# Three hand-placed reorderings in the start of a fused soft-cap attention and max-out MLP: a w2 product ahead of the next transposes, three w1 parts ahead of the first crossbar transpose, fill units behind the second quad's values

## The chip, the cores and the metric

The kernel runs on one core of one Trainium2 chip. The metric is the device time of one execution in microseconds (us). Five runs of the kernel before gave 344.70, 344.70, 343.57, 343.85 and 345.86 us, a median of 344.7. Beside these, one execution was profiled: every duration and every wait below comes from its trace. A page of that trace names lines of the kernel (L426 is line 426) and engines: PE does matrix multiplies, PEld loads their weights, DVE, ACT and POOL work on elements, SP issues DMAs.

## The reference

Attention over 8 batches of 12 heads, 448 rows and 64 columns, with capped scores; its output, laid out as 3584 rows of 768, goes through two up-projections, of which the larger is kept, and one down-projection:

```python
scores = cap * np.tanh(scale * (q @ k.T) / cap)
attn = np.exp(scores); attn = attn / attn.sum(-1)
x = attn @ v
h1, h2 = x @ w1, x @ w2
out = np.maximum(h1, h2) @ w_out
```

The kernel uses max(h1, h2) = h2 + relu(h1 - h2). So it needs two matrices that depend on the weights alone: wd = w1 - w2, for the relu part, and wm = w2 @ w_out, which takes x straight to the h2 part of the output. It computes out = x @ wm + relu(x @ wd) @ w_out.

## The kernel before

**Attention.** Two heads make a pair, two pairs a quad; there are 24 quads, t = 0 to 23, three to a batch. Three pairs are one group g for loading: `load` brings k, q and v, `cast` turns them into bf16 (on DVE or POOL), and then k and q have to be transposed into the tile `qkT`. For g = 0 and 1 PE does it, a pair at a time (`transposes(i)`, L281 and L282, and a copy on DVE, L283). From g = 2 on one DMA does it for the whole group, through the crossbar: `cross(g)`, L287, issued by SP when POOL has finished the group's casts. `cross(2)` serves quad 3 on, and `cross(3)` is wanted first by `scores(4, 1)`.

For a quad, `scores(t, p)` multiplies k with q (L309, L312) and has ACT take the tanh (L313). Parts 0 and 1 have three score tiles each, j = 0 to 2, part 2 has one, and each tile is two banks of PSUM. `ex` takes the exp (L318). `total(t)` sums it with ones as weights (L352, L356, later L359), and DVE turns the sums into reciprocals `inv` (L361, L363, L365). `values(t)` multiplies with v (L375, L381), and `normalize(t)` scales the result on DVE into `xT` (L396). The pool `s_psum` has two buffers, for score tiles and totals alike; `v_psum` has one, for values and, where the code says `v_psum`, for a third score tile. `expo` has two buffers, so `ex(2, 0)` must wait until `total(0)` and `values(0)` have read what quad 0 left.

**The fill.** Everything else that PE does is cut into units of one matmul and put into a queue, `fill_q`. `F(n)` in the hand-written order runs n units at that place. The first 144 units make wm: `(c, T)` is eight transposes of slice c of w2 (L241) and a copy on DVE into `w2T` (L243), and `(c, half)` is eight matmuls with w_out (L252) and a copy on DVE (L256). After them come the units of `moe(b)`, one generator per batch: 48 units of the up-projection with wd (L408, each six followed by the relu on DVE, L413), and then 14 units (six L423 with wm, eight L426) for each half row block of the output, followed by a copy on DVE (L429). `moe(b)` is put into the queue only when its batch's last quad is normalized, so `F` finds the queue empty if the units run out before. Inside the loop over t = 3 to 23 a quad asks for 47 units. `moe(0)` has 132 units, and `moe(1)` is put in at the end of t = 5.

**wd.** w1 comes as twelve parts of 256 KB, `load_w1(c, part)` (L228), issued by SP; w2 comes through POOL's queue (L220). `subtract(c, part, eng)` (L232) makes wd, part 0 for the first four column blocks f, part 1 for the last four. POOL has c = 2 to 5 of part 0 ahead of `cast(3, "k")` and `cast(3, "q")`, and c = 0 to 2 of part 1 behind them; DVE has the rest.

**The queues.** Every engine takes its instructions in the order of the code. SP's order around the change is: q and k of group 2, v of group 1, two parts of w1, `cross(2)`, four parts of w1, k and q of group 3, six parts of w1 (part 1), and, later in the code, `cross(3)`, v of groups 2 and 3, k and q of groups 4 and 5.

Of the kernel before, what the change touches and what calls it, by code (L numbers as in the profile page):

```python
# [10 lines left out]
def kernel(  # L11
# [22 lines left out]
    KC, FC = DM // P, DF // P  # L34
# [40 lines left out]
    def flat(g):  # L75
        return kqf[g % 2].rearrange("p n j c -> p n (j c)")
# [22 lines left out]
    def half(b):  # L99
        return slice(0, 64) if b % 2 == 0 else slice(64, P)  # L100
# [8 lines left out]
    def raw_of(g, what):  # L109
        if (g, what) not in raw:  # L110
            raw[g, what] = raw_tile(what)
        t = raw[g, what]
        m = t[:, : 2 * L * NJ * D].rearrange("p (h c) -> p h c", c=NJ * D)
        l = t[:, 2 * L * NJ * D :].rearrange("p (h d) -> p h d", d=D)
        return t, m, l
# [28 lines left out]
    def cast(eng, g, what, n0=0, n1=L, halves=(0, 1)):  # L144

        b = g * L // NP
        x, m, l = raw_of(g, what)
        if what == "v" and g < NT:

            x = x[:, : L * S].rearrange("p (n c) -> p n c", c=S)  # L150
            for h in halves:
                r = slice(64 * h, 64 * h + 64)
                for a in range(2):
                    eng.tensor_copy(
                        vp[g % 2][64 * a : 64 * a + 64, h::2, :, :].rearrange("p n j d -> p n (j d)"),
                        x[r, :, NJ * D * a : NJ * D * (a + 1)],
                    )
                eng.tensor_copy(vl[g % 2][r, :, r], x[r, :, 2 * NJ * D :])  # L158
            return
        if what == "v":  # L160
            eng.tensor_copy(  # L161
                vp[g % 2][:, 2 * n0 : 2 * n1, :, :].rearrange("p h j d -> p h (j d)"), m[:, 2 * n0 : 2 * n1, :]
            )
            for par in range(2):
                r = slice(64 * par, 64 * par + 64)
                eng.tensor_copy(vl[g % 2][r, n0:n1, r], l[r, n0:n1, :])
            return
        if g < NT:

            x = x[:, n0 * S : n1 * S].rearrange("p (n c) -> p n c", c=S)  # L170
            if what == "q":
                eng.tensor_copy(flat(g)[:, n0:n1, Q0 : Q0 + S], x)
                return
            eng.tensor_copy(flat(g)[:, n0:n1, : NJ * P], x[:, :, : NJ * P])
            for par in range(2):
                r = slice(64 * par, 64 * par + 64)
                eng.tensor_copy(kf[g % 2][r, n0:n1, 3, r], x[r, :, NJ * P :])
            return
        o = b % 2 if what == "q" else 0
        t = (kf if what == "k" else qf)[g % 2]  # L180
        eng.tensor_copy(
            t[:, n0:n1, o : o + NJ, :].rearrange("p n j (h d) -> p n h j d", h=2),
            m[:, 2 * n0 : 2 * n1, :].rearrange("p (n h) (j d) -> p n h j d", h=2, d=D),
        )
        if what == "q":
            eng.tensor_copy(
                t[half(b), n0:n1, 3 * (1 - o), :],
                l[half(b), 2 * n0 : 2 * n1, :].rearrange("p (n h) d -> p n (h d)", h=2),
            )
        else:  # L190
            for par in range(2):
                r = slice(64 * par, 64 * par + 64)
                eng.tensor_copy(t[r, n0:n1, 3, r], l[r, n0:n1, :])
# [70 lines left out]
    def qkT_of(g):  # L264
        if g not in qkT:
            qkT[g] = stage.tile([P, L, 8, P], bf16, name="qkT")
        return qkT[g]

    def transposes(i):

        g, n = divmod(i, L)
        ps = mm_psum.tile([P, 512], f32, name="mm").bitcast(bf16)
        x = flat(g)[:, n, :]

        todo = [(j * D, (j % 3) * P + (j // 3) * 64) for j in range(6)]
        odd = i // NP % 2
        todo += [(Q0 + j * D, Q0 + (64 * j if not odd else 0 if j == 6 else 64 + 64 * j)) for j in range(R7)]
        for c, to in todo:
            for a in range(2):
                r = slice(64 * a, 64 * a + 64)  # L280
                nc.tensor.transpose(ps[r, to : to + 64], x[r, c : c + D], ident[r, r])  # L281
        nc.tensor.transpose(ps[:, NJ * P : Q0], x[:, NJ * P : Q0], ident)  # L282
        nc.vector.tensor_copy(qkT_of(g)[:, n, :, :].rearrange("p j c -> p (j c)")[:, : Q0 + S], ps[:, : Q0 + S])  # L283
# [12 lines left out]
    def scores(t, p, last=None, js=None):  # L296

        if (t, p) not in tanh:
            tanh[t, p] = att.tile([P, 2 * NJ, S], bf16, name="tanh")
        for j in js or range(NJ if p < 2 else 1):  # L300
            s = two_banks(last if last and j == NJ - 1 else s_psum)
            for m in range(2):
                i = 2 * t + (p if p < 2 else m)
                g = i // L
                k0 = qkT[g][:, i % L, :, :].rearrange("p j c -> p (j c)")
                o = Q0 + (64 * (i // NP % 2) if g >= NT else 0)
                qTn = k0[:, o : o + S]
                if p == 2:
                    nc.tensor.matmul(s[:, m, :S], k0[:, 3 * P : 4 * P], qTn)  # L309
                else:  # L310
                    r = slice(64 * m, 64 * m + 64)
                    nc.tensor.matmul(s[:, m, :S], k0[r, j * P : (j + 1) * P], qTn[r, :])  # L312
            nc.scalar.activation(tanh[t, p][:, 2 * j : 2 * j + 2, :], s[:, :, :S], AF.Tanh, scale=scale / cap)  # L313

    def ex(t, p):
        n = 2 * NJ if p < 2 else 2
        expo[t, p] = att.tile([P, n, S], bf16, name=f"expo{p}", bufs=2)
        nc.scalar.activation(expo[t, p], tanh[t, p][:, 0:n, :], AF.Exp, scale=float(cap))  # L318

    def e_of(t, ab, j):  # L320
        return expo[t, ab][:, 2 * j : 2 * j + 2, :]
# [24 lines left out]
    def total(t):  # L346

        ss = two_banks(s_psum)[:, 0, :]
        if t < NS:
            for j in range(NJ):  # L350
                for ab, h, r in HEADS:
                    nc.tensor.matmul(  # L352
                        ss[r, :S], ones[:, :32], e_of(t, ab, j)[:, h, :], start=(j == 0), stop=False
                    )
            for ab, h, r in HEADS:
                nc.tensor.matmul(ss[r, :S], ones2[:, h, :32], expo[t, 2][:, ab, :], start=False, stop=True)  # L356
        else:
            for ab, h, r in HEADS:
                nc.tensor.matmul(ss[r, :S], ones[:, :32], esum[t][:, 2 * ab + h, :], start=True, stop=True)  # L359
        st = att.tile([P, NB, 32], f32, name="st", bufs=1)  # L360
        nc.vector.transpose(st.rearrange("p b c -> p (b c)"), ss[:, :S])  # L361
        rs = att.tile([P, NB, 1], f32, name="rs", bufs=2)
        nc.vector.reciprocal(rs, st[:, :, 0:1])  # L363
        inv[t] = att.tile([P, S], f32, name="inv", bufs=2)
        nc.vector.transpose(inv[t].rearrange("p (b c) -> p b c", c=32), rs.to_broadcast([P, NB, 32]))  # L365
# [88 lines left out]
    def F(n):  # L454
        rate[1] += n * rate[0]
        while rate[1] >= 1 and fill_q:
            g = fill_q[0]
            if g is not rate[2]:
                rate[2] = g
                next(g)  # L460
            rate[1] -= 1
            try:
                next(g)
            except StopIteration:
                fill_q.pop(0)
        if not fill_q:
            rate[1] = 0.0
# [30 lines left out]
    def w2wo(*parts):  # L498
        for c, half in parts:
            fill_q.append(turn_w2(c) if half is None else premultiply(c, half))  # L500

    T = None
    w2wo((0, T), (1, T), (0, 0), (2, T), (1, 0), (2, 0), (0, 1), (1, 1), (3, T), (2, 1), (3, 0), (4, T), (3, 1))
    w2wo((4, 0), (5, T), (4, 1), (5, 0), (5, 1))

    fill_const(nc.vector, 0)
# [34 lines left out]
    cast(nc.gpsimd, 2, "k")  # L541
    cast(nc.gpsimd, 2, "q")
    cast(nc.gpsimd, 1, "v", halves=(1,))
    scores(0, 2)
    ex(0, 2)
    F(28)
    scores(1, 0, v_psum)
    ex(1, 0)
    F(28)
    scores(1, 1, v_psum)  # L550
    ex(1, 1)
    F(24)
# [1 line left out]
    cast(nc.vector, 0, "v", halves=(0,))  # L554
    scores(1, 2)
    ex(1, 2)
    for c in range(2):
        load_w1(c, 0)
    cross(2)
    for c in range(2, KC):  # L560
        load_w1(c, 0)
    load(3, "k")
    load(3, "q")
# [4 lines left out]
    x0 = values(0)  # L568
    scores(2, 0, js=(2,))
    ex(2, 0)  # L570
    transposes(5)
    total(0)
    F(8)
    scores(2, 1, js=(0, 1))
    normalize(0, x0)
    F(4)
    scores(2, 1, js=(2,))
    cast(nc.vector, 1, "v", halves=(0,))
    F(4)
    scores(2, 2)  # L580
    ex(2, 1)
    F(8)
    total(1)
    normalize(1, values(1))
    F(2)

    scores(3, 0, v_psum)
    ex(2, 2)
# [11 lines left out]
    load(3, "v")  # L600
    extra(4)
    extra(5)
    F(4)
    for c in range(2):
        subtract(c, 0, nc.vector)
    total(2)
# [88 lines left out]
```

## Time and profile before

| what | us |
|---|---|
| median of five runs | 344.7 |
| the profiled execution, its own time | 344.41 |
| its span, first to last instruction | 342.6 |
| PE busy in the span | 323.6 (94%) |
| ACT busy | 277.2 (81%) |
| DVE busy | 232.1 (68%) |
| POOL busy | 107.2 (31%) |

The granted clock of PE was 1.00 of full speed over the span. The profile has several views. The busy row gives each engine's share of the span. A table of stretches gives the same for any part of it. A timeline lists one engine's instructions in order of time: the start, the time that a run of equal instructions took, the engine, line and tile names, the count and, in brackets, how long the engine had been idle before and what ended that. The DMA view gives, for each issue, the time from the issue to the landing of its data.

### The profile page before, as it was taken

What the parts mean: (1) busy time and instruction counts of PE and PEld (TensorE: products, weight loads), DVE (VectorE), ACT (ScalarE), POOL (GpSimd) and SP (SyncE); (2) the same over time, 40 slices, a digit from 0 to 9 for tenths busy, and PEclk for the clock granted to TensorE, in tenths of its full rate; (3) what the DMA queues carried; (4) which work ended last, traced back from release to release, by engine and by line L of the source; (5) the groups of instructions that cost most, each with busy time, mean ns of one, the idle gap of its engine ahead of it and who ended that gap; (6) DMA issues with size and microseconds to landing.
All of it is one profiled execution on the core that took longest, in us unless ns stands there. A gap on an engine that the chain in (4) does not pass through costs nothing.

```text
span 342.6 us, 6835 instructions
## 1 busy us (share of the span) xinstructions
PE 323.6 (94%) x2722; PEld 163.3 (48%) x2722; DVE 232.1 (68%) x417; ACT 277.2 (81%) x241; POOL 107.2 (31%) x180
## 2 busy tenths in 40 slices
PE   3799969799999999999999999999999999999995
PEld 1555424345444554455445554445445544555563
DVE  4546765587887677677686668777776877874321
ACT  2999969789999999899989999999989999900000
POOL 8334667274134214403412441342144130000000
PEclk9999999999999999999999999999999999999999
DMA  7999799999996879686986689749955920012022
GB/s 217 199 238 302 192 265 272 231 250 232 185 279 175 209 196 277 161 174 140 265 229 126 125 222 309 170 130 232 294 118 142 227 78 27 0 48 92 2 92 92
DMA packets 106047, 61.78 MB, mean 180 GB/s; under 512 B 62624, under 2 KB 101024, under 8 KB 106016
## 3 DMA queue, kind: packets, MB, share of 16 engines
q1 hardware_dynamic: 102144, 58.21, 67.1%
q0 software_dynamic: 3872, 3.15, 5.9%
q8 instruction: 21, 0.34, 0.4%
q14 instruction: 10, 0.08, 0.1%
HBM read 42.47 MB, written 11.01 MB: 156 GB/s over the span
## 4 chain that ended last, share of the span: by engine, by line
PE 80%; DMA 10%; DVE 4%; POOL 2%; SPq 2%; issue 1%; POOLq 0%; DVEq 0%
PE mm L426 22%; PE mm L408 19%; PE mm L423 16%; PE v L375 6%; PE s L312 6%; DMA gT<-in_moe_w_dram 3%; DMA vr<-in_v_dram 3%; DMA qr<-in_q_dram 2%; PE v L312 2%; PE v L381 2%; PE s L309 2%; PE mm L252 2%; PE s L359 2%; DMA qkT<-kqf 2%; SPq L133 1%
## 5 line engine op out<-in xcount | busy, mean ns | idle before, releaser
L318 ACT ACTIVATE expo<-tanh 128x2688 bf16<-128x2688 bf16 (+1 forms) x72 | 140.3, 1950 | 0.7 <-PE s L352 0.5
L313 ACT ACTIVATE tanh<-s 128x896 bf16<-128x896 f32 x123 | 107.4, 914 | 20.9 <-PE s L312 17.8
L426 PE MATMUL mm<-wo_sb,gT 128*128 128x384 bf16 x448 | 86.0, 327 | 0.0
L408 PE MATMUL mm<-xT,wd_sb 128*128 128x448 bf16 x384 | 78.2, 353 | 1.0 <-DVE gT L413 0.7
L423 PE MATMUL mm<-wm_sb,xT 128*128 128x384 bf16 x336 | 66.0, 327 | 0.0
L429 DVE COPY osb<-mm 128x384 f32<-128x384 f32 x56 | 31.1, 555 | 44.2 <-PE mm L426 43.8
L426 PEld LDWEIGHTS <-gT 128*128 128x128 bf16 x448 | 42.3, 98 | 34.6 <-issue 8.5
L408 PEld LDWEIGHTS <-wd_sb 128*128 128x128 bf16 x384 | 35.8, 98 | 39.5 <-issue 9.0
L413 DVE TENSOR_SCALAR gT<-mm 128x448 bf16<-128x448 f32 x64 | 39.4, 621 | 20.5 <-PE mm L408 20.3
L423 PEld LDWEIGHTS <-xT 128*128 128x128 bf16 x336 | 31.8, 98 | 25.9 <-issue 5.9
L655 POOL COPY mark<-inv 1x1 f32<-1x1 f32 x18 | 3.2, 177 | 130.6 <-DVE inv L365 114.9
L313 ACT ACTIVATE tanh<-v 128x896 bf16<-128x896 f32 x45 | 41.6, 925 | 0.0
L375 PE MATMUL v<-expo,vp 128*32 128x448 bf16 x576 | 35.9, 353 | 0.0
L312 PE MATMUL s<-qkT 64*128 64x448 bf16 x198 | 28.3, 363 | 6.4 <-DMA qkT<-kqf 4.4
L396 DVE TENSOR_TENSOR xT<-v,inv 128x448 bf16<-128x448 f32 x48 | 27.7, 619 | 3.0 <-DVE inv L365 0.5
L338 DVE TENSOR_TENSOR esum<-expo 128x896 bf16<-128x896 bf16 x40 | 27.8, 695 | 0.0
L340 DVE TENSOR_TENSOR esum<-esum,expo 128x896 bf16<-128x896 bf16 x40 | 25.7, 643 | 0.8
L361 DVE STREAM_TRANSPOSE st<-s 128x448 f32<-128x448 f32 x24 | 15.6, 649 | 14.7 <-PE s L359 12.6
L336 DVE TENSOR_TENSOR esum<-esum,expo 64x896 bf16<-64x896 bf16 x40 | 24.6, 616 | 1.1
L312 PEld LDWEIGHTS <-qkT 64*128 64x128 bf16 x288 | 10.5, 95 | 28.4 <-issue 16.0
L375 PEld LDWEIGHTS <-vp 128*32 128x32 bf16 x576 | 15.4, 97 | 10.6 <-DVE vl L158 0.4
L161 POOL CAST vp<-vr 128x1152 bf16<-128x1152 f32 x14 | 16.0, 1144 | 10.3 <-DMA vr<-in_v_dram 10.1
(66 smaller groups left out, 261.7 us busy)
## 6 DMA issues: line engine op xcount, KB each, us to landing
kr<-in_k_dram SPq DMA_DIRECT2D x14, 576.0 KB, 7.1
qr<-in_q_dram SPq DMA_DIRECT2D x14, 576.0 KB, 7.5
vr<-in_v_dram SPq DMA_DIRECT2D x14, 576.0 KB, 4.9
out_dram<-osb SPq DMA_DIRECT2D x20, 384.0 KB, 4.1
out_dram<-osb SPq DMA_DIRECT2D x16, 192.0 KB, 3.7
osb<-in_moe_w_dram SPq DMA_DIRECT2D x8, 256.0 KB, 5.9
gT<-in_moe_w_dram POOLq DMA_DIRECT2D x12, 128.0 KB, 9.2
wo_sb<-in_moe_w_out_dram POOLq DMA_DIRECT2D x4, 384.0 KB, 8.7
```

Of the source, the lines that this page charges most:

```text
L312: nc.tensor.matmul(s[:, m, :S], k0[r, j * P : (j + 1) * P], qTn[r, :])
L313: nc.scalar.activation(tanh[t, p][:, 2 * j : 2 * j + 2, :], s[:, :, :S], AF.Tanh, scale=scale / cap)
L318: nc.scalar.activation(expo[t, p], tanh[t, p][:, 0:n, :], AF.Exp, scale=float(cap))
L338: nc.vector.tensor_add(d, e_of(t, ab, 0), e_of(t, ab, 1))
L340: nc.vector.tensor_add(d, d, e_of(t, ab, 2))
L375: nc.tensor.matmul(ps[r, :S], vp[g % 2][:, 2 * n + h, j, u::2], e_of(t, ab, j)[:, h, :], start=(j == 0), stop=False,)
L396: nc.vector.tensor_mul(x_of(t, u), ps[:, u, :S], inv[t])
L408: nc.tensor.matmul(ps[:, :S], wd_sb[:, c, f * P : (f + 1) * P], x[:, c, cs], start=(c == 0), stop=(c == KC - 1))
L413: nc.vector.tensor_relu(g[f // FH][:, f % FH, cs], ps[:, :S])
L423: nc.tensor.matmul(ps[:, : DM // 2], x[:, c, ts], wm_sb[:, c, hs], start=(c == 0), stop=False)
L426: nc.tensor.matmul(ps[:, : DM // 2], g[f // FH][:, f % FH, ts], wo_sb[:, f, hs], start=False, stop=(f == FC - 1))
L429: nc.vector.tensor_copy(osb[:, hs], ps[:, : DM // 2])
```

## The change

All edits are in the hand-written order; no instruction is added or removed.

- In the list of w2 products `(0, 0)` stands ahead of `(1, T)`.
- Eight fill units are taken ahead of `scores(0, 2)`; the next `F(28)` becomes 16, and the one after it 32.
- Three parts of w1 instead of two are issued ahead of `cross(2)`.
- `total(0)` stands ahead of `transposes(5)`.
- The fill between the scores of quad 2 changes from 4 and 4 units to 6 and 2.
- The eight units ahead of `total(1)` go, and the fill behind `normalize(1)` grows from 2 to 10.
- The fill ahead of the first two subtracts on DVE and `total(2)` grows from 4 to 8.

```diff
-    w2wo((0, T), (1, T), (0, 0), (2, T), (1, 0), ...
+    w2wo((0, T), (0, 0), (1, T), (2, T), (1, 0), ...
...
+    F(8)
     scores(0, 2)
     ex(0, 2)
-    F(28)
+    F(16)
     scores(1, 0, v_psum)
     ex(1, 0)
-    F(28)
+    F(32)
     scores(1, 1, v_psum)
...
-    for c in range(2):
+    for c in range(3):
         load_w1(c, 0)
     cross(2)
-    for c in range(2, KC):
+    for c in range(3, KC):
         load_w1(c, 0)
...
+    total(0)
     transposes(5)
-    total(0)
     F(8)
     scores(2, 1, js=(0, 1))
     normalize(0, x0)
-    F(4)
+    F(6)
     scores(2, 1, js=(2,))
     cast(nc.vector, 1, "v", halves=(0,))
-    F(4)
+    F(2)
     scores(2, 2)
     ex(2, 1)
-    F(8)
     total(1)
     normalize(1, values(1))
-    F(2)
+    F(10)
 
     scores(3, 0, v_psum)
...
-    F(4)
+    F(8)
     for c in range(2):
         subtract(c, 0, nc.vector)
     total(2)
```

## The prediction

> **What bounds the kernel now.** I read the busy row first, then a table of stretches, then PE's timeline where the table shows gaps, and from each gap back to what ended it.
>
> ```profile
> PE 323.6 (94%) x2722; PEld 163.3 (48%) x2722; DVE 232.1 (68%) x417; ACT 277.2 (81%) x241; POOL 107.2 (31%) x180
> ```
>
> PE comes first. The stretches (length, then busy time of PE, PEld, DVE, ACT, POOL, clock, DMA share, GB/s) say where its other 19 us are:
>
> ```profile
> 62.30:92.00 29.70, 29.67 (x266) 14.76 (x266) 21.68 (x36) 27.81 (x24) 11.54 (x18) 1.00 1.06 232
> 92.00:297.00 205.00, 203.98 (x1658) 99.31 (x1651) 152.93 (x272) 196.77 (x173) 61.00 (x102) 1.00 0.73 182
> ```
>
> From 62.3 us on PE idles 0.03 and 1.02 us; ACT has 10 us to spare there. So the time is *when PE leaves its start-up at 62.3* plus the work still left then. The whole change lies before 62.3. PE's timeline there, gaps in brackets:
>
> ```profile
> 44.40 0.55 PE L312 MATMUL s<-qkT 64*128 64x448 bf16 x4 [1.51 <-DMA qkT<-kqf]
> ...
> 47.01 0.82 PE L252 MATMUL mm<-wo_sb,w2T 128*128 128x384 bf16 x4
> 49.23 0.75 PE L352 MATMUL s<-expo,ones 128*32 128x448 bf16 x12 [1.40 <-ACT tanh L313]
> ...
> 56.27 3.20 PE L408 MATMUL mm<-xT,wd_sb 128*128 128x448 bf16 x16
> 62.33 0.55 PE L312 MATMUL s<-qkT 64*128 64x448 bf16 x4 [2.86 <-DMA qkT<-kqf]
> ```
>
> Three stalls: S1, scores(3,0) waits for the first crossbar; S2, total(2) waits for a score buffer that ACT's tanh frees; S3, scores(4,1) waits for the second crossbar. S3 comes last and is largest: PE is there at 59.47, the data at 62.3. Whatever makes PE earlier or later before 59.5 changes S3, not the end. Only two things reach the end: **the landing of cross(3)**, and **units done earlier that PE then need not do later**. The landing's history, on POOL and SP:
>
> ```profile
> 52.28 1.14 POOL L181 CAST kqf<-kr 128x1152 bf16<-128x1152 f32 x1 [0.79 <-PE v L381]
> 53.36 0.75 POOL L193 CAST kqf<-kr 64x192 bf16<-64x192 f32 x2
> 54.96 1.15 POOL L181 CAST kqf<-qr 128x1152 bf16<-128x1152 f32 x1 [0.85 <-DMA qr<-in_q_dram]
> 56.17 0.51 POOL L186 CAST kqf<-qr 64x384 bf16<-64x384 f32 x1
> ```
>
> ```profile
> 30.91 3.48 SPq L228 DMA_DIRECT2D osb<-in_moe_w_dram  x2
> 38.73 3.76 SPq L287 DMA_TRANSPOSE qkT<-kqf  x1
> 42.54 1.06 SPq L228 DMA_DIRECT2D osb<-in_moe_w_dram  x2
> ...
> 46.39 0.60 SPq L128 DMA_DIRECT2D qr<-in_q_dram  x1
> ...
> 56.70 4.01 SPq L287 DMA_TRANSPOSE qkT<-kqf  x1
> ```
>
> q of group 3 is issued at 46.39 and takes 8.4 us (DMA view): it lands at 54.8, POOL casts it until 56.68, SP issues cross(3) at 56.70, and that takes 5.6 us, to 62.3. (The wait put to PE at 52.28 is the landing of k: its large DMA, issued at 44.59, takes 7.5 us.)
>
> **The change, part by part.**
>
> *w2 order and F(8), 16, 32.* Units done before scores(1,0) go from 28 to 24; before scores(1,1) both have 56, and after F(24) 80. scores(0,2) moves behind eight transposes: from 14.40 to about 15.1, as twelve took 1.37 us. ACT takes it at 17.34, so this is covered for 2 us. (0,0) must now wait for the DVE copy of (0,T), some 0.7 us, of which scores(0,2) hides 0.6; in exchange the 0.31 us wait of (1,T) at 16.82 for w2 goes. scores(1,0) is ready by 18.7 as before, ACT wants it at 19.13. **0.**
>
> *total(0) ahead of transposes(5).* ex(2,0) waits 0.51 us for total(0) (ACT, 34.53); that goes. But transposes(5) comes 0.95 us later (L352 and L356, 33.67 to 34.6), and its DVE copy stands behind three DVE steps of total(0) (0.65+0.24+0.65), so scores(2,1) is 0.3 to 0.5 us later than 35.95. ACT meets it at 36.4 either way. **0**, and its cover is S1.
>
> *F(6), F(2), and F(10) behind values(1).* total(1) needs the buffer of the third score tile of quad 2's second pair, whose tanh ends at 39.5 (third of four from 36.88): it moves from 39.70 to 39.4 at best. values(1) needs v of group 1, cast by POOL and DVE until 41.0 (39.12+1.59, 40.66+0.35), and ends at 42.4 as now. Then ten units instead of two: eight transposes (0.6) and two L252 (0.3), so PE is at scores(3,0) at 43.3, while the crossbar lands at 44.3. **0**; S1 shrinks to 1.0. On DVE normalize(1) now stands ahead of the w2T copy (0.67 us), which removes the 0.20 us wait at 45.15. This lands in S2.
>
> *F(8) ahead of total(2).* Four more units of 0.165 us (0.82 us for four less overlap) = 0.66 us of work inside the 1.40 of S2. PE's arrival at S3 does not change: 59.47. But DVE's copy of (5,0) now comes ahead of two subtracts, so these start near 49.0 instead of 47.1 and end by 51.3; normalize(2) ends some 0.5 us later than 53.3. The first moe unit that reads its result is the fifth, near 54.5. **0.**
>
> *Do the four units count?* PE leaves S3 with 26 units of moe(0) done instead of 22. But moe(0) has 132 units, and until the end of t = 5 the queue gets nothing else: quads 3 to 5 ask for 132 before moe(1) is put in and find 126 now, 122 after. The loss is at the end of t = 5. There DVE decides:
>
> ```profile
> 87.80 0.56 DVE L429 COPY osb<-mm 128x384 f32<-128x384 f32 x1 [0.60 <-PE mm L426]
> 88.27 0.62 DVE L340 TENSOR_TENSOR esum<-esum,expo 128x896 bf16<-128x896 bf16 x1
> 88.99 1.27 DVE L336 TENSOR_TENSOR esum<-esum,expo 64x896 bf16<-64x896 bf16 x2
> 90.29 0.56 DVE L429 COPY osb<-mm 128x384 f32<-128x384 f32 x1
> ```
>
> total(5) starts at 90.34, right behind the two L336. With four units fewer PE's last unit is done at 89.2 instead of 89.9, but the last L429 then stands *between* the L336, waits for that unit, and the second L336 ends at 89.25+0.5+0.6 = 90.4. total(5) is where it was. **0**; bounds 0 and -0.66.
>
> *Third w1 part ahead of cross(2).* SP is free from 34.39 to 38.73, when POOL's cast releases cross(2): the issue, about 0.5 (1.06 for two at 42.54), is free. The engines are free too: their DMA share is 0.45 from 36.5 to 38.0 and 0.13 from 38.0 to 39.9, two engines of 16. But those two are what a landing waits for: the w1 parts issued at 30.9 and 34.0 land at 39.7 and 40.5. The third would land near 41.2.
>
> [...] The row says otherwise: cross(3) takes 5.6 us although the last w1 part before it lands at 59.3 (54.35+4.9), 2.5 us after its issue; for cross(2) that is 1.7 us now and 2.5 after, and it takes 5.6 too. I take the row, cross(2) at 44.3. [...]
>
> After cross(2) SP issues one part less (0.57 us), and the engines carry 256 KB less ahead of q of group 3. What that is worth on the late engines: nothing, if they only carry it earlier and start late; 0.7 us by the landings of parts at 39.7 and 40.5, or 56.0 and 56.6; 1.2 to 1.5 by those at 45.3, 46.8 and 48.0. The late engines have the time of the crossbar to recover in, and SP's issue gains 0.5, so I take **-0.6**: q lands at 54.2, cross(3) is issued at 56.1, lands at 61.7. Ends 0 and -1.3. POOL is ready for it (its subtracts end before 51 as their data come earlier). From there all later loads stand behind cross(3) on SP and move with it; cross(4) lands at 83.0, scores(6,0) runs at 83.2, and both shift alike.
>
> **Sum.** -0.6 us: 344.41 becomes 343.8 on the profiled execution. The median lies 0.3 above that, so 344.1; I give 344.0.
>
> **The rivals.**
>
> *A, the forecast (0.55):* S3 ends 0.6 us earlier, the rest is swallowed: 344.0.
>
> *B, both count (0.20):* the late engines gain 1.2 us, and the four units survive t = 5 (0.66), because DVE's L429 comes early enough: 344.7-1.9 = 342.8. For it: the spacing at 45 to 48, and PE leads DVE there. Against: the L429 between the L336.
>
> *C, the third part does nothing (0.13):* the late engines are the bound from 34 to 55 and only swap their order; S3 ends at 62.3: 344.7.
>
> *D, wd is late, slower (0.12):* with 26 units done, PE meets wd's part 1 of c = 3 to 5 right behind scores(4,1), from 62.5, instead of near 64.0, and its three subtracts on DVE now stand behind the fourth L413 (about 59.7). The first took 1.39 us beside POOL, the others 0.64 each. At 0.64 they end at 61.7 and nothing waits; at 1.39 they end at 63.9, and PE stands 1.5 us: 344.7-0.6+1.5 = 345.6. It makes the kernel slower from an end after 63.0 on. Against: POOL's three subtracts (3.38 us from 56.1) end at 59.5.
>
> **How the numbers follow.** No change is what lies within 0.5% (1.7 us), about what a measurement of this kernel can tell. Faster by more is most of B and a little of A, 0.21; slower by more is the tail of D and costs I don't see, 0.11; the rest, 0.68. The range goes from a little under B to D, 342.5 to 345.6.
>
> **What would show it.** After: one line of three L228 before L287; cross(2) lands near 44.3; S1 near 1.0, S2 near 0.7; L181 of q at 54.3, cross(3) at 56.1, S3 near 2.2 ending at 61.7; a new gap of 0.8 us ahead of total(5). It is wrong if PE leaves S3 at 62.3 or after, if no gap shows at total(5), or if an L408 behind S3 waits for wd.

## The result, and the profile after

The changed kernel took 344.47 us (median of 44 executions, 342.31 to 346.48), the kernel before 345.06 us beside it (79 executions, 342.56 to 348.14). The ratio is 0.9984, with a 95% interval of 0.9971 to 0.9997: 0.55 us less, where 0.6 was forecast. It is a small gain, inside what the prediction called no change; the interval reaches from 0.1 to 1.0 us. The experiments below trace it to the step that the prediction named. But the profile after also holds something that the prediction had left out.

PE's timeline of the changed kernel, in the columns used before, at the three stalls and at total(5):

```profile
42.93 0.55 PE L312 MATMUL s<-qkT 64*128 64x448 bf16 x4 [1.09 <-DMA qkT<-kqf]
...
47.76 0.75 PE L352 MATMUL s<-expo,ones 128*32 128x448 bf16 x12 [0.82 <-ACT tanh L313]
...
61.09 0.55 PE L312 MATMUL s<-qkT 64*128 64x448 bf16 x4 [2.71 <-DMA qkT<-kqf]
...
90.03 0.36 PE L359 MATMUL s<-esum,ones 128*32 128x448 bf16 x1
91.02 0.37 PE L359 MATMUL s<-esum,ones 128*32 128x448 bf16 x3 [0.63 <-DVE esum L336]
```

S1 went from 1.51 to 1.09 and S2 from 1.40 to 0.82, because fill units now stand in them. S3 ends at 61.09 instead of 62.33. At total(5) there is a new gap of 0.63 us, which waits for an L336 on DVE. SP's timeline has the three w1 parts in one line ahead of the first crossbar:

```profile
31.38 1.82 SPq L228 DMA_DIRECT2D osb<-in_moe_w_dram  x3
37.21 4.04 SPq L287 DMA_TRANSPOSE qkT<-kqf  x1
...
45.95 0.60 SPq L128 DMA_DIRECT2D qr<-in_q_dram  x1
...
54.75 4.29 SPq L287 DMA_TRANSPOSE qkT<-kqf  x1
```

This whole execution had started faster (the scores of quad 0's second pair ran at 10.04 instead of 11.20, on the arrival of the first loads), so a single pair of profiles does not tell how much of the 1.24 us is the change's.

And yet the span is 343.3 us, longer than the 342.6 of before. From scores(4,1) to the end it takes 282.2 us here and 280.3 there. The table of stretches says why (columns as before: the length, busy us of PE, PEld, DVE, ACT and POOL, then the granted clock):

```profile
58.40:61.10 2.70, 0.01 (x2) 0.01 (x2) 2.06 (x4) 0.57 (x1) 0.00 (x0) 1.00 1.08 183
62.20:65.60 3.40, 3.40 (x11) 1.41 (x10) 0.87 (x2) 3.40 (x4) 1.49 (x3) 0.50 0.95 270
```

PE stands still for 2.7 us, and then its clock is at 0.50 for one stretch of 3.4 us. What that costs is seen in the 22 matmuls behind scores(4,1), first before and then after:

```profile
63.00 4.34 PE L408 MATMUL mm<-xT,wd_sb 128*128 128x448 bf16 x22
```

```profile
61.76 6.02 PE L408 MATMUL mm<-xT,wd_sb 128*128 128x448 bf16 x22
```

They take 1.7 us longer. The profiled execution of before, with a stall just as long, kept a clock of 1.00; the last section shows where the two differ.

### The profile page after: what moved, and what is told of

Same layout as the page of the kernel before. It is cut to its first block, busy times and chain, and to the rows that moved or that the text cites. A ratio compares the mean times of both kernels' runs of the same rounds, so it can differ in the third digit from the quotient of the medians.

```text
span 343.3 us, 6835 instructions
## 1 busy us (share of the span) xinstructions
PE 325.7 (95%) x2722; PEld 164.4 (48%) x2722; DVE 230.6 (67%) x417; ACT 277.1 (81%) x241; POOL 105.6 (31%) x180
## 4 chain that ended last, share of the span: by engine, by line
PE 79%; DMA 9%; SPq 5%; DVE 3%; POOL 2%; issue 1%; POOLq 0%; DVEq 0%
PE mm L426 22%; PE mm L408 19%; PE mm L423 16%; PE v L375 6%; PE s L312 6%; DMA gT<-in_moe_w_dram 3%; PE v L312 2%; PE v L381 2%; PE s L309 2%; DMA osb<-in_moe_w_dram 2%; SPq L139 2%; DMA qr<-in_q_dram 2%; DMA qkT<-kqf 2%; PE s L359 2%; SPq L228 1%
## 5 line engine op out<-in xcount | busy, mean ns | idle before, releaser
L408 PE MATMUL mm<-xT,wd_sb 128*128 128x448 bf16 x384 | 79.9, 358 | 1.1 <-DVE gT L413 0.7
L408 PEld LDWEIGHTS <-wd_sb 128*128 128x128 bf16 x384 | 36.4, 99 | 40.8 <-issue 11.0
L338 DVE TENSOR_TENSOR esum<-expo 128x896 bf16<-128x896 bf16 x40 | 25.8, 645 | 0.0
L336 DVE TENSOR_TENSOR esum<-esum,expo 64x896 bf16<-64x896 bf16 x40 | 24.6, 616 | 1.2
L252 PE MATMUL mm<-wo_sb,w2T 128*128 128x384 bf16 x96 | 17.9, 327 | 0.5 <-DVE w2T L243 0.3
```

Source lines behind the costliest of these rows:

```text
L338: nc.vector.tensor_add(d, e_of(t, ab, 0), e_of(t, ab, 1))
L408: nc.tensor.matmul(ps[:, :S], wd_sb[:, c, f * P : (f + 1) * P], x[:, c, cs], start=(c == 0), stop=(c == KC - 1))
```

## The experiments

Each runs beside executions of the kernel before. T is the start of scores(4,1), where S3 ends; the last column is the span less T. In e6, e10 and e11 the matmuls without use stand ahead of S3, and S3 is what idle time is left behind them. "Dips" counts executions with a mean clock under 0.997, which one stretch of 3.4 us at 0.50 suffices for; the count does not say where that stretch lies. In e2's profile it lies at 17.55 us, in the start-up, and not behind S3.

| kernel | ratio (95%) | median us | dips | T | S3 | span less T |
|---|---|---|---|---|---|---|
| before (first profile) | 1 | 344.7 | - | 62.33 | 2.86 | 280.3 |
| changed | 0.9984 (0.9971 to 0.9997) | 344.47 | 22 of 44 | 61.09 | 2.71 | 282.2, dip |
| e1 before again | 0.9993 (0.9971 to 1.0014) | 344.71 | 14 of 22 | 61.62 | 3.30 | 281.7, dip |
| e2 w1 edit alone | 0.9960 (0.9941 to 0.9978) | 343.37 | 13 of 22 | 60.57 | 0.40 | 280.5 |
| e3 all but the w1 edit | 1.0002 (0.9976 to 1.0028) | 344.96 | 6 of 14 | 61.28 | 1.83 | 280.6 |
| e4 five parts | 0.9968 (0.9946 to 0.9990) | 343.80 | 8 of 15 | 60.45 | 0.18 | 281.2 |
| e5 four units undone | 0.9985 (0.9962 to 1.0008) | 344.44 | 12 of 22 | 60.63 | 1.76 | 280.7 |
| e6 twelve idle matmuls | 0.9988 (0.9971 to 1.0004) | 344.71 | 1 of 22 | 61.57 | none | 280.5 |
| e7 w1 edit, two parts later | 0.9999 (0.9982 to 1.0017) | 344.97 | 9 of 22 | 61.13 | 0.66 | 282.8 |
| e8 changed again | 0.9978 (0.9957 to 0.9999) | 343.98 | 11 of 22 | 61.59 | 2.50 | 282.2, dip |
| e9 w1 edit alone, again | 0.9966 (0.9947 to 0.9985) | 343.96 | 13 of 22 | 61.62 | 2.72 | 282.0, dip |
| e10 w1 edit, six idle matmuls | 0.9961 (0.9942 to 0.9980) | 343.52 | 6 of 22 | 61.04 | 1.74 | 280.6 |
| e11 changed, six idle matmuls | 1.0002 (0.9975 to 1.0029) | 344.98 | 1 of 14 | 61.10 | 1.06 | 282.2 |
| e12 four parts, old fill | 0.9918 (0.9892 to 0.9943) | 342.60 | 4 of 10 | 59.89 | 0.49 | 280.3 |

### Where the gain sits: e2, e3, e8, e9

e2 is the kernel before with

```diff
-    for c in range(2):
+    for c in range(3):
         load_w1(c, 0)
     cross(2)
-    for c in range(2, KC):
+    for c in range(3, KC):
         load_w1(c, 0)
```

> The kernel before with the third w1 part ahead of the first crossbar transpose and nothing else. Theory (only the landing of the second crossbar reaches the end): all of the gain, ratio about 0.998, q of group 3 lands about 10.0 us behind the landing of the first crossbar (10.5 before), no new gap ahead of total(5). Rival (the reordered fill makes the gain): ratio 1.000.

e3 is the changed kernel with these lines as they were.

> The changed kernel with two w1 parts ahead of the first crossbar, as before. Theory: ratio 1.000; the stall of scores(4,1) ends as late as before (about 18 us behind the landing of the first crossbar), the stall of total(2) is near 0.8, and a gap of about 0.6 us stands ahead of total(5). Rival (the reordered fill makes the gain, four units done earlier are kept): ratio 0.998 and no such gap.

The w1 edit alone gives 0.9960, everything else together 1.0002. e3's interval by itself would still admit 0.998, but e2, which has the fill of before, excludes that the fill alone makes the gain. In e3 the reordered fill does what it does in the changed kernel, and PE's waits from 42 to 100 us show both sides of it: S2 at 0.8, and the 0.6 us ahead of total(5) (in us: total, times, longest):

```profile
PE s L312 <- DMA qkT<-kqf: 2.9, 2, 1.8
PE s L352 <- ACT tanh L313: 0.8, 1, 0.8
PE s L359 <- DVE esum L336: 0.6, 1, 0.6
```

So shorter S1 and S2 bring nothing. T is 62.33, 61.62 and 61.28 in the three profiles without the w1 edit (mean 61.74), and 61.09, 61.59, 60.57, 61.62, 60.63, 61.04 and 61.10 in seven with three parts (changed, e8, e2, e9, e5, e10, e11; mean 61.09; e6, where PE itself was late, and e7, which moves other loads too, are left out): 0.65 us. But each is one execution, they scatter by half a microsecond, and part of the difference is how fast each one started. The issue of the first crossbar waits for POOL's cast of group 2 (in the changed kernel's profile the cast ends at 37.19 and the issue is at 37.21) and not for the w1 parts, so the edit cannot bring it forward. Counted from there, in us (means):

| w1 parts ahead of the first crossbar | q of group 3 issued | its transfer takes | it has landed | second crossbar has landed |
|---|---|---|---|---|
| 2 (before, e1, e3) | 7.8 | 8.2 | 16.1 | 23.5 |
| 3 (the nine other profiles) | 7.9 | 7.8 | 15.7 | 23.4 |
| 4 (e12) | 8.1 | 6.5 | 14.6 | 22.1 |
| 5 (e4) | 7.1 | 6.7 | 13.8 | 22.5 |

With each part moved q lands earlier, with four and five parts (one profile each) outside the range of the others. For three parts the row shows 0.3 us for q and 0.2 for the second crossbar, less than the scatter within the group (15.0 to 16.3, and 22.5 to 23.8). So the profiles show the path of the gain, but its size for three parts rests on the times of the many executions. In e2 q of group 3 lands 9.9 us behind the first crossbar, where 10.0 was expected; but the profiles without the edit have 10.5, 10.9 and 9.9 (e3), so that one figure tells little, and in e3 the second crossbar lands 17.4 us behind the first, not the expected 18.

e2 came out better than the whole change, so both were run again.

> The changed kernel, unchanged, on the same chip and beside the same executions of before as the others. Theory: ratio 0.998, between 0.997 and 0.9995; the second crossbar lands 0.6 to 1.2 us earlier than in the profiles of before (62.3 and 61.6), and a gap of about 0.63 us stands ahead of total(5). If the w1 edit alone is really better than the whole change, it stays above 0.997.

> The kernel of the w1 edit alone once more. If it is really better than the whole change, its ratio is 0.996 again and its interval stays under 0.998. If the two are the same and the first figure was a draw, it comes to 0.997 to 0.9985, as the changed kernel (0.9984 and 0.9978).

0.9978 and 0.9966. e8 has the gap at total(5), but its second crossbar landed at 61.55, as late as in e1 (61.58), against what was expected. Of e9 neither answer holds. Its figure is near 0.996, but the interval reaches 0.9985 and overlaps both of the changed kernel. Whether the reordered fill takes back some tenths of the gain stays open.

A rival is that the gain is only a matter of PE's clock. Executions with a clock of 0.997 or more, compared alone, speak against it: their mean is 343.43 in e8 (11 executions), and 344.03 in before beside it (24), 0.6 us less, give or take 0.5. The same comparison gives 1.0 us less for e2, 0.5 less for e9 and 0.2 more for e3. Over all executions e8's mean is 0.9 us lower, so about a third of its gain goes with fewer dips.

### The four units: e5

e5 is the changed kernel with `F(4)` instead of `F(8)` ahead of total(2).

> The changed kernel with four fill units instead of eight ahead of total(2), as before. Theory (the four units done earlier only move an idle stretch): the 0.63 us gap ahead of total(5) goes, the stall of total(2) grows from 0.8 to about 1.4, and the time stays as that of the changed kernel, ratio 0.998, within 0.2 us of it. Rival (the four units count): 0.6 us slower, ratio near 1.000. Rival the other way (the fill and its order of copies on DVE cost something): faster, ratio 0.996 like the w1 edit alone.

S2 is back at 1.47, the gap ahead of total(5) is gone, and the ratio is 0.9985 against 0.9984. These intervals are wider than the 0.66 us at stake; the traces are closer. From T to the end e5 takes 280.7 us, and e3, with the four units, 280.6. Four units done earlier were worth nothing: they moved an idle stretch of 0.65 us from 47 to 90 us. DVE's timeline of the changed kernel shows how it comes back:

```profile
88.55 0.62 DVE L336 TENSOR_TENSOR esum<-esum,expo 64x896 bf16<-64x896 bf16 x1
89.76 0.56 DVE L429 COPY osb<-mm 128x384 f32<-128x384 f32 x1 [0.59 <-PE mm L426]
90.35 0.62 DVE L336 TENSOR_TENSOR esum<-esum,expo 64x896 bf16<-64x896 bf16 x1
```

Before, the two L336 stood side by side, with the copy behind them. Now PE's last unit of moe(0) comes between them in the order of the code, its copy stands between them on DVE and waits for PE, and the second L336, for which total(5) waits, waits for the copy.

### More parts ahead of the crossbar: e4, e12

e4 is the changed kernel with five parts ahead of `cross(2)`.

> The changed kernel with five w1 parts instead of three ahead of the first crossbar. Theory: SP and most DMA engines are free there, so two more parts bring q of group 3 another 1.0 to 1.3 us earlier; the first crossbar lands up to 1 us later, which lengthens the stall of scores(3,0) and shortens that of scores(4,1), and the end gains about 1 us more: ratio near 0.995. Rival (the late engines only swap their order): the second crossbar lands where it did, ratio 0.998.

The expected 1 us more did not come: 0.9968. q of group 3 did land earlier, as the table above shows, but now both crossbars are slow. The first takes 7.1 us from issue to landing, so S1 grows from 1.09 to 2.65 us; the second is issued at 53.65, a microsecond earlier than in the changed kernel, and takes 6.8. T is 60.45, and S3 is 0.18: PE is now late itself. Behind it an L408 waits 0.24 us for wd.

e12 moves four parts and leaves the fill of before alone.

> The kernel before with four w1 parts instead of two ahead of the first crossbar, nothing else. If each part moved is worth 0.6 to 0.7 us, the second crossbar lands at 60.3 and the ratio is 0.996. If the gain is used up with the third, because the late DMA engines then still carry w1 part 1 when the second crossbar is issued (its time from issue to landing grew from 5.6 to 6.3 us in a profile of the changed kernel and to 6.8 with five parts), the ratio is that of three, 0.9965 to 0.998, and the time from issue to landing is over 6 us.

This is the best kernel of all: 342.60 us, ratio 0.9918. SP's timeline (start, time, count):

```profile
31.31 2.64 SPq L228 DMA_DIRECT2D osb<-in_moe_w_dram  x4
37.75 4.39 SPq L287 DMA_TRANSPOSE qkT<-kqf  x1
...
45.83 0.60 SPq L128 DMA_DIRECT2D qr<-in_q_dram  x1
...
54.27 4.07 SPq L287 DMA_TRANSPOSE qkT<-kqf  x1
```

and PE's at the ends of S1 and S3:

```profile
44.33 0.55 PE L312 MATMUL s<-qkT 64*128 64x448 bf16 x4 [1.74 <-DMA qkT<-kqf]
...
59.89 0.55 PE L312 MATMUL s<-qkT 64*128 64x448 bf16 x4 [0.49 <-DMA qkT<-kqf]
```

The first crossbar takes 6.5 us, longer than the 5.7 and 5.6 with three parts in the changed kernel, but S3 has room for that; the second is issued at 54.27, lands in 5.6 us, and T is 59.89, 1.85 us earlier than the mean without the edit. S3 is nearly used up. The ratio makes 2.8 us of it and the means 2.5 (342.52 against 345.06), more than T shows. Most of the rest goes with the clock. Among executions with a clock of 0.997 or more e12's mean is 342.36 (6 executions) and that of before 343.81 (13): 1.45 us. The 42 dips of before have a mean of 345.44, the 4 of e12 one of 342.76, so before loses about 1.2 us to dips and e12 0.2. That rests on ten executions. The expectation that the gain ends with the third part, read from the slow second crossbar of one profile, was wrong.

### A load behind the crossbar: e7

```diff
-    for c in range(KC):
+    for c in range(4):
         load_w1(c, 1)
...
     cross(3)
+    for c in range(4, KC):
+        load_w1(c, 1)
```

> The kernel before with the third w1 part ahead of the first crossbar, and the last two of the six part-1 loads of w1 issued behind the second crossbar instead of ahead of it. If the second crossbar waits on the late DMA engines for the w1 parts issued ahead of it, its landing comes up to 1 us earlier (near 59.5 to 60) and its time from issue is 5.6 us. But the last two subtracts of wd are then done near 62 to 63, so an L408 of the fifth column block waits up to 1 us behind scores(4,1): ratio 0.996, as the w1 edit alone, between 0.994 and 0.998. If the crossbar does not depend on those parts, nothing lands earlier and the wait for wd is added: ratio 0.998 or above.

The second crossbar landed no earlier: POOL's cast of q sets its issue, 0.03 us behind the cast, and it took 5.5 us, where most took 5.5 to 5.8. What came was the wait for wd, the mechanism of rival D:

```profile
61.80 1.50 PE L408 MATMUL mm<-xT,wd_sb 128*128 128x448 bf16 x7
64.83 0.36 PE L408 MATMUL mm<-xT,wd_sb 128*128 128x448 bf16 x1 [1.53 <-DVE wd_sb L232]
```

PE stands 1.53 us at the first matmul that needs the late subtract, and the gain of the w1 edit is gone (0.9999).

### The clock: e1, e6, e10, e11

> The kernel before, unchanged, run as if it were a change, so that its single executions show their granted clock. All theories: ratio 1.000. If the 0.16% of the change is a matter of the clock of PE (a dip to half speed behind the stall on the second crossbar), the executions of before should show a mean clock under 0.997 clearly more often than the 26 of 44 of the changed kernel. If the gain is the earlier landing of the second crossbar, the share of dips is about the same, and executions at clock 1.000 alone differ by about 0.6 us.

14 of 22 dips. (The 26 of 44 in this text was a miscount; it is 22.) All executions of before that ran beside e2 to e12, in three series, have 130 of 190, 68%; the changed kernel, in its two series, has 33 of 66. So before dips more often, 68% against 50%, and its S3 was longer in the profiles, 2.86 and 3.30 us against 2.71 and 2.50. The 0.6 us at clock 1.000 alone, which the second theory asked for, is what e8 shows above.

e6 puts matmuls without use into S3:

```diff
+        if t == 3:
+            warm = mm_psum.tile([P, 512], f32, name="mm")
+            for _ in range(12):
+                nc.tensor.matmul(warm[:, : DM // 2], ident,
+                    wo_sb[:, 0, : DM // 2], start=True, stop=True)
         if more:
             scores(t + 1, 1, v_psum)
```

> The changed kernel with twelve matmuls more, whose result nothing reads, ahead of scores(4,1): about 1.95 us of PE work inside its stall on the second crossbar, with no other change. If the stall is what brings PE's clock to half speed behind it, fewer executions have a mean clock under 0.997 (22 of 44 for the changed kernel), and the median comes near that of its executions at full clock, 343.8. If the clock does not depend on that stall, the share stays near one half and the median at 344.5; it is slower by up to 2 us if the stall is shorter than the added work.

Dips fall from one half to 1 of 22: in the changed kernel S3 is what brings nearly all of them. But the median is 344.71, not the expected 343.8. The twelve end at 61.5 in the profile, 0.3 us behind the landing of the crossbar, so part of what they save they take. It is not all: at a clock of 0.997 or more e6's mean is 344.79, 1.4 us above that of e8 beside it. What makes the other microsecond is not shown. e10 and e11 use six, on e2 and on the changed kernel.

> The w1 edit alone, with six matmuls whose result nothing reads ahead of scores(4,1): 1.0 us of PE work in a stall of about 2.2 us. Profiles so far had the clock dip behind stalls of 2.5 us and more and none behind 1.8 us and less, so the share of executions under a clock of 0.997 falls from 13 of 22 to a few, and as the work fits into the stall, the mean falls by half of the 1.65 us that a dip costs: ratio near 0.995. If the dips are not worth that much, it stays at that of the w1 edit alone.

> The changed kernel with six matmuls more instead of the twelve of the earlier run, which cut the dips from 22 of 44 to 1 of 22 but gained no time. If the twelve gave back their gain by outlasting the stall (1.95 us and a wait of 0.34 us for their buffer), six keep most of it: dips in 5 of 22 or fewer, ratio 0.996. If the dips cost nothing, ratio 0.998.

The dips fall again, to 6 of 22 and 1 of 14. The times do not follow: 0.9961 against 0.9960 and 0.9966 for e2 and e9, and 1.0002 for e11, where 0.996 was expected. e11's profile has another wait, 1.59 us of scores(6,0) for the third crossbar, which landed at 83.5; in the changed kernel PE met it with nothing to wait for. One execution does not say whether the added matmuls bring that about. So: behind S3 a dip costs 1.2 to 1.7 us (span less T of changed, e1, e8 and e9, against 280.5 in the undisturbed profiles), idle matmuls bring the share of dips down to 1 of 22, 6 of 22 and 1 of 14, and no version shown here got faster by that.

## Why the prediction was right, point by point

**Only what S3 hands on counts.** Right. From T to the end seven profiles (before, e2, e3, e5, e6, e10, e12) take 280.3 to 280.7 us, whatever the fill looks like; the others have a dip behind S3 or, in e4, e7 and e11, waits of 0.24, 1.53 and 1.59 us of their own, which make most of what e11 and e7 take longer, but not of what e4 does. The edits to w2's order, to total(0), to the fill and to total(2) give 1.0002 together (e3, 0.9976 to 1.0028).

**The landing of cross(3), -0.6 us.** Right in the path: in all 14 profiles POOL's cast of q starts 0.15 us behind q's landing, and the crossbar is issued 0.03 us behind the cast; four and five parts bring q 1.4 and 2.2 us earlier. The size fits: 0.55 and 0.76 us by the two ratios, 0.6 at full clock. But the intervals reach from almost nothing to 1 us and more, and the profiles alone show 0.2 to 0.65, so that 0.6 was hit so closely is in part luck. One step did not come out: the prediction had SP's issue of q gain 0.5 us. Behind the first crossbar q is issued after 7.9 us with three parts and 7.8 with two. What became shorter is its transfer, 8.2 to 7.8 us, and 6.5 with four parts, which fits with 256 KB less, for each part moved, issued between the crossbar and q.

**The crossbar behind the third part.** The row held: cross(2) took 5.7 and 5.6 us in the two profiles of the changed kernel, with the last w1 part landing 2.5 and 2.2 us behind its issue. But behind a later tail the crossbar took longer. Over all 14 profiles and both crossbars, the time from the crossbar's issue to its landing, by how long after that issue the last w1 part ahead of it lands:

| last w1 part after the issue | crossbar takes |
|---|---|
| 1.4 to 2.5 us (15 cases) | 5.5 to 5.8 us |
| 2.6 to 3.0 us (10 cases) | 5.5 to 6.3 us |
| 3.2 us (e12, first) | 6.5 us |
| 3.6 and 4.0 us (e4, first and second) | 7.1 and 6.8 us |

With a tail of up to 2.5 us no crossbar took more than 5.8 us, from 3.2 us on none took less than 6.5, and between the two it was now one and now the other. What makes it longer is not shown. The prediction's choice was right for three parts; for four and five the first crossbar took 6.5 and 7.1 us.

**S1, S2 and S3.** Forecast 1.0, 0.7 and 2.2 us; measured 1.09, 0.82 and 2.71 (2.50 in e8). In the changed kernel's profile the second crossbar took 6.3 us, not 5.6, which would be S3's excess; but e8's took 5.6 and S3 was still 2.50, so a part is scatter between executions.

**The four units.** Right, with its reason: forecast a gap of 0.8 us at total(5), measured 0.63 and gone with e5.

**What it did not have.** The sum took PE's clock as 1.00 throughout, because the profile of before showed that. In half or more of the executions it is not so (33 of 66 of the changed kernel, 130 of 190 of before). The forecast of 0.6 us was therefore right for the landing, but S3's length has a second price that no term of the sum held. In e8 it was about a third of the gain; in e12 it was some 1.1 of 2.5 us.

## What to carry to other kernels

Find the last stall of the start-up and what ends it: work moved about ahead of it changes stalls, not the end, and one transfer moved into an idle stretch of the queue was worth more than all the edits of the fill together (ratios 0.9960 and 0.9966 against 1.0002). Before a fill unit is moved forward, ask when the queue next runs dry, for in this kernel the idle time came back there (0.63 us at total(5)). And try such a move in steps: with the fill of before three parts gave 0.9960 and 0.9966 and four 0.9918; with the new fill three gave 0.9984 and 0.9978 and five 0.9968. Each step brought q of group 3 earlier (16.1 us behind the issue of the first crossbar with two parts, 15.7, 14.6 and 13.8 with three, four and five) and, from the fourth part on, a slower first crossbar (6.5 and 7.1 us from issue to landing).

## What the hardware showed that was not expected

After S3 the clock of PE went to 0.50 for one stretch of 3.41 us in four profiles (stalls of 2.50, 2.71, 2.72 and 3.30 us), but not after the 2.86 us of before, nor where S3 was 1.83 us or less. The traces record when the granted clock changes, and within each trace all these changes lie a whole number of steps of 3.413 us apart (in the changed kernel's 14, 15 and 96 steps behind the first, in that of before 96). Cut into windows of that length, counted from the first change, the two profiles differ: in that of before a boundary falls into the stall; in the changed kernel's the stall lies within one window:

```profile
57.10:60.51 3.41, 2.37 (x13) 1.01 (x11) 2.39 (x3) 3.33 (x4) 3.03 (x3) 1.00 1.03 203
60.51:63.93 3.42, 1.60 (x11) 0.72 (x12) 1.71 (x4) 1.14 (x2) 0.00 (x0) 1.00 0.87 180
```

```profile
58.76:62.17 3.41, 1.08 (x9) 0.44 (x10) 1.70 (x3) 0.83 (x2) 0.00 (x0) 1.00 1.01 213
62.17:65.58 3.41, 3.41 (x11) 1.42 (x10) 0.85 (x2) 3.41 (x4) 1.47 (x3) 0.50 0.94 270
```

Before, PE idles for 1.04 us in one window and 1.82 in the next, and keeps its clock. In the changed kernel it idles for 2.33 us of one window, and the next has half the clock. In these two profiles, from the first record of a full clock on, two windows are followed by half the clock: this one and the last full one of the changed kernel's, with 2.49 us of idle PE; all others within the two spans had 1.82 us or less and were not. Over the 14 profiles the windows that were followed by half the clock had 2.1 us or more, and those that were not 1.9 us or less. So in these profiles two stalls of nearly the same length, 2.86 and 2.71 us, differ in the clock behind them by where they fell. e2's stretch at 17.55 fits too: two waits for w2 in the start-up make 2.29 us of idle PE in one window. What in the chip does this is not shown.

Part of the spread of single executions, 342.3 to 346.5 us, goes with the dips: in the changed kernel's two series the clock and the time go together (correlation -0.78 and -0.80), while in e6, with one dip in 22, the times still spread over 3.5 us.
